# Two matrix layers that read their moving operand's 512 columns from two halves in turn

## The chip, the core and the metric

The kernel runs on one core of a Trainium2 chip. The engines named below are PE (TensorE: matmuls; its weight loads are listed apart as PEld), DVE (VectorE), ACT (ScalarE), POOL (GpSimd) and SP (SyncE, which issues the DMAs). The metric is the device time of one launch in microseconds, the median of several runs.

## What is computed

A linear recurrence over time (batch 4, 8 heads, 768 steps, 48 features per head) feeds a two-layer perceptron of 3072 tokens, 384 model features and 2048 hidden units:

```python
for t in range(S):
    cur = einsum('bhd,bhe->bhde', u * k[t], v[t])
    y[t] = einsum('bhd,bhde->bhe', r[t], state + cur)
    state = w * state + einsum('bhd,bhe->bhde', k[t], v[t])
x = y.transpose(0, 2, 1, 3).reshape(B * S, H * D)     # 3072 x 384
h = x @ w_in                                          # 3072 x 2048
g = 0.5 * h * (1 + erf(h / sqrt(2)))
out = g @ w_out                                       # 3072 x 384
```

## The kernel before

Time is cut into 6 chunks of 128 steps. A chunk has 4 x 128 = 512 tokens, and they are the 512 columns of every matmul of the perceptron, in the order batch, then time. The recurrence of a chunk is worked out in closed form for 4 pairs of heads ("groups", with the tiles `Tb`, `Nb`, `Am`, `Sa`, `Sb`, `cs` and the PSUM tiles `A` and `Y`). A group ends in `xx` (or `x3`), the perceptron's input of that chunk.

The hidden units are cut into 16 blocks of 128. One step m is one block of one chunk, 96 steps in all. Each factor is split into a high and a low part in the 4-byte type fp32r, and three products are added up: high x high, high x low, low x high. A step is therefore

- `product1`, 9 matmuls of 512 columns (3 products x 3 pieces of the 384 features) that add up in the PSUM tile `Hp`;
- on ACT, two passes of Gelu over `Hp`: `gh` (line 728, rounded to fp32r) and `gf` (line 729); on DVE `gl` = `gf` - `gh` (line 730);
- `product2`, 9 matmuls of 512 columns that read `gh` and `gl` and add up in the PSUM tiles `O0`, `O1`, `O2`. In the last chunk `O2`'s 512 columns are done as two matmuls of 256, the second half into `Y`.

On PE, `product2` of step m-1 stands behind `product1` of step m, so that Gelu is worked out under it. `Hp` is one tile: the next `product1` must wait until `gf` has read it. The weights (`wh`, `wl`) are loaded as 8-byte numbers and split once, in the 16 steps of the first chunk: on ACT lines 395, 398 and 404, on DVE lines 400 and 407. In that chunk DVE and ACT so do the weights' split beside Gelu and the next chunk's groups.

The order of all instructions is worked out before the launch by a planner (`Plan`). It holds a list of operations with an engine, an estimated duration, a due time and dependencies, and plays them through; what it starts first on an engine stands first in that engine's queue. `MM` is its duration of one matmul of 512 columns; it has no other use. The last line of `kernel` puts the output, written as chunk x feature x column, back in the order of tokens.

Of the kernel before, what the change touches and what calls it, by code (L numbers as in the profile page):

```python
# [21 lines left out]
B, H, S, D = 4, 8, 768, 48  # L22
DM, DF = 384, 2048
C = 128
NCH = S // C
# [14 lines left out]
FIRST, STEP, STEP_LAST = 27000, 8400, 3900  # L40
WEIGHT_AHEAD, GROUP_AHEAD, GROUP_DUE = 26000, 28000, 18000
LEFT = 6
HEATS, HEAT_NS, HEAT_ROOM, MM = 10, 300, 100, 233
WIDE = 96
POOL_DUE, POOL_CLASH = 8000, 550
LATER_BONUS = "d"
# [144 lines left out]
def rwkv_gelu_mlp(tc, rkT, rkv, wuT, uN, wmlp, r, k, vT, w, u, out):  # L191
    nc = tc.nc
    with ExitStack() as ctx:
# [61 lines left out]
        act = lambda n: 60 + n / 1.2  # L255
        pool = lambda n: 200 + n * 2.1

        flat2 = lambda x: x.rearrange("p a b c -> p (a b c)")
        slot = lambda gi: gi if gi < NP else NP + gi % 2

# [432 lines left out]
        def product1(x, j, n, ks=range(3), start=False, stop=False, dst=Hp):  # L693
            wt, a = ((wh, 0), (wl, 0), (wh, 1))[n]
            for k_ in ks:
                nc.tensor.matmul(dst, lhsT=wt[j][:, 0, k_ * 128:(k_ + 1) * 128], rhs=x[:, a, k_, :],  # L696
                                 start=start and k_ == ks[0], stop=stop and k_ == ks[-1])

        def hidden(m):
# [8 lines left out]
        def moe1(m, at):  # L708
            t, j = divmod(m, NJ)
            high, low, GH, GL = hidden(m)  # L710
            x, X = xx[t % 2], f"xx{t % 2}"

            xr = lambda a, ks=range(3): [f"{X}{k_}{a}" for k_ in ks]
            gaps = [f"{X}{k_}g{i}" for k_ in range(3) for i in range(2)]
            n1 = 2 * j
            dst, H_ = (O[2], "O2") if m == 1 else (Hp, "H")
            if m == 0:
                gaps0 = lambda k_: gaps[2 * k_:2 * k_ + 2]
                for k_ in range(3):
                    first = add("pe", 3 * MM, at + k_, lambda k_=k_: [  # L720
                        product1(x, j, n, (k_,), k_ == 0 and n == 0, k_ == 2 and n == 2) for n in range(3)],
                        r=["wh0", "wl0"] + xr("h", (k_,)) + xr("l", (k_,)) + gaps0(k_), w=["H"])
                    plan.heat_to = plan.heat_to or first
            else:
                for n in range(3):
                    add("pe", 3 * MM, at + n, lambda n=n: product1(x, j, n, start=n == 0, stop=n == 2, dst=dst),
                        r=[f"{('wh', 'wl', 'wh')[n]}{n1}"] + xr("hhl"[n]) + gaps, w=[H_])
            add("act", 480, LATER, lambda: nc.scalar.activation(out=high, in_=dst, func=AF.Gelu, scale=256.0), r=[H_], w=[GH])  # L728
            add("act", 480, LATER, lambda: nc.scalar.activation(out=gf, in_=dst, func=AF.Gelu, scale=256.0), r=[H_], w=["gf"])  # L729
            add("dve", dve(512), LATER, lambda: nc.vector.tensor_tensor(  # L730
                out=low, in0=gf, in1=high.bitcast(F32), op=ALU.subtract), r=["gf", GH], w=[GL], port=True)
# [5 lines left out]
        def product2(j, high, low, n, part):  # L737
            wt, gt = ((wh, high), (wl, high), (wh, low))[n]
            d, dst, a, b = part
            nc.tensor.matmul(dst[:, a:b], lhsT=wt[j][:, 1, d * 128:(d + 1) * 128], rhs=gt[:, a:b],  # L740
                             start=(j == 0 and n == 0), stop=(j == NJ - 1 and n == 2))

        def moe2(m, at, dest):
# [4 lines left out]
            def go(m, n, which, at):  # L748
                j = m % NJ
                high, low, GH, GL = hidden(m)  # L750
                add("pe", MM * sum(parts[i][3] - parts[i][2] for i in which) / TOK, at, lambda: [product2(j, high, low, n, parts[i]) for i in which],
                    r=[f"{('wh', 'wl', 'wh')[n]}{2 * j + 1}", (GH, GH, GL)[n]], w=[banks[i] for i in which])
# [164 lines left out]
        with tc.If(plain[0] < LP * NP):  # L917
            general = ctx.enter_context(ExitStack())
            xT = general.enter_context(tc.tile_pool(name="xT", bufs=1, space=bass.MemoryType.DRAM)).tile(
                [3, 128, NB, S], F32, name="xT")  # L920
            with ExitStack() as rec:
                recur(rec.enter_context(tc.tile_pool(name="rec", bufs=1)), xT)
            g = general.enter_context(tc.tile_pool(name="g", bufs=2))
            with tc.For_i(0, NCH, 1) as c:
                xf = g.tile([128, 3, NB, C], F32, name="xf")
                xhl = g.tile([128, 2, 3, TOK], F32R, name="xhl")
                for k_ in range(3):
                    nc.scalar.dma_start(xf[:, k_], xT[k_][:, :, ds(c * C, C)])
                xflat = xf.rearrange("p k b t -> p k (b t)")
                nc.scalar.copy(out=xhl[:, 0], in_=xflat)  # L930
                nc.vector.tensor_tensor(out=xhl[:, 1], in0=xflat, in1=xhl[:, 0].bitcast(F32), op=ALU.subtract)
                o = g.tile([128, 3, TOK], F32, name="og")
                for j in range(NJ):
                    for n in range(3):
                        product1(xhl, j, n, start=n == 0, stop=n == 2)
                    ghs, gfs, gls = (g.tile([128, TOK], dt, name=x) for x, dt in (("ghs", F32R), ("gfs", F32), ("gls", F32R)))
                    nc.scalar.activation(out=ghs, in_=Hp, func=AF.Gelu, scale=256.0)
                    nc.scalar.activation(out=gfs, in_=Hp, func=AF.Gelu, scale=256.0)
                    nc.vector.tensor_tensor(out=gls, in0=gfs, in1=ghs.bitcast(F32), op=ALU.subtract)
                    for n in range(3):  # L940
                        for part in PARTS:
                            product2(j, ghs, gls, n, part)
                for d in range(3):
                    nc.vector.tensor_scalar(out=o[:, d], in0=O[d], scalar1=256.0, scalar2=None, op0=ALU.mult)
                nc.scalar.dma_start(out[ds(c, 1)].rearrange("o d p n -> p (o d) n"), o)
            general.close()
# [61 lines left out]
```

## Time and profile before

| | |
|---|---|
| median of 3 runs | 478.93 us (478.82 to 479.67) |
| profiled execution, first to last instruction | 476.6 us |
| time outside the span, median less span | 2.3 us |
| PE busy | 469.2 us, 98% |
| DVE, ACT, POOL busy | 230.7, 181.8, 67.6 us |
| DMA | 46.6 MB, 98 GB/s in the mean |

The profile holds one execution; no device time of its own is given for it beside the span. A matmul's listed duration (393 to 398 ns for 512 columns) covers its whole way through the array and overlaps with the next one's. What a matmul costs in a stream is the distance from its start to the next one's start, which the timeline's start times give.

### The profile page before, as it was taken

The page shows a single profiled execution, that of the slowest core. Times are in us where ns is not written, and L with a number is a line of the kernel's source. Part 1 is how long each engine was busy: PE and PEld are TensorE (multiplying, and loading weights), DVE is VectorE, ACT ScalarE, POOL GpSimd, SP SyncE. Part 2 cuts the span into 40 slices and gives each one's busy share as a digit, 9 for nine tenths or more (in the row PEclk, how much of TensorE's full clock was granted, in tenths as well). Part 3 has the DMA queues.
Part 4 walks back from the last instruction along what each step waited for, and adds up shares of the span by engine and source line. Part 5 has one row for each costly group of instructions (what it writes and reads, how often), then busy time and mean ns, then how long its engine had stood idle before and what let it go on. Part 6 is the DMA issues. An engine that isn't in the chain of part 4 may idle for free.

```text
span 476.6 us, 10284 instructions
## 1 busy us (share of the span) xinstructions
PE 469.2 (98%) x4525; PEld 378.3 (79%) x4525; DVE 230.7 (48%) x345; ACT 181.8 (38%) x333; POOL 67.6 (14%) x91
## 2 busy tenths in 40 slices
PE   8999999999999999999999999999999999999996
PEld 6767788888888787888888888888888887888875
DVE  7989989754354266153543543544435311211111
ACT  9998897233222223222223222223322222322221
POOL 1331021221020222010202202202112000000000
PEclk9999999999999999999999999999999999999999
DMA  8978682414023034031231330321402000100002
GB/s 306 362 296 312 231 265 91 122 48 155 25 83 106 2 114 153 1 106 39 69 106 67 96 99 9 106 54 52 162 15 91 14 0 12 66 1 1 1 0 72
DMA packets 15426, 46.60 MB, mean 98 GB/s; under 512 B 3664, under 2 KB 4048, under 8 KB 15376
## 3 DMA queue, kind: packets, MB, share of 16 engines
q1 hardware_dynamic: 15376, 45.88, 28.8%
q8 instruction: 37, 0.61, 0.5%
q14 instruction: 13, 0.11, 0.1%
HBM read 38.73 MB, written 4.72 MB: 91 GB/s over the span
## 4 chain that ended last, share of the span: by engine, by line
PE 92%; DMA 4%; ACT 3%; issue 0%; DVE 0%; ACTq 0%
PE Hp L696 42%; PE O L740 41%; PE Y L606 2%; DMA E<-W 2%; PE A L614 2%; PE Y L634 2%; PE A L623 1%; DMA raw<-in_wmlp_dram 1%; PE Y L740 1%; ACT W L344 0%; ACT Sa L530 0%; ACT wa L312 0%; ACT L291 0%; ACT wa L395 0%; ACT gh L728 0%; ACT gf L729 0%
## 5 line engine op out<-in xcount | busy, mean ns | idle before, releaser
L696 PE MATMUL Hp<-xx,wh 128*128 128x512 f32 x570 | 167.2, 401 | 0.0
L730 DVE TENSOR_TENSOR gl<-gf,gh 128x512 fp32r<-128x512 f32 x92 | 66.9, 727 | 166.4 <-ACT gf L729 166.1
L728 ACT ACTIVATE gh<-Hp 128x512 fp32r<-128x512 f32 x91 | 54.4, 598 | 213.9 <-PE Hp L696 213.8
L696 PEld LDWEIGHTS Hp<-xx,wh 128*128 128x128 f32 x570 | 104.4, 188 | 25.8 <-ACT gf L729 1.5
L696 PE MATMUL Hp<-xx,wl 128*128 128x512 f32 x285 | 82.1, 395 | 0.0
L740 PE MATMUL O<-gh,wh 128*128 128x512 f32 (+1 forms) x276 | 78.6, 391 | 0.5 <-ACT gf L729 0.5
L740 PE MATMUL O<-gh,wl 128*128 128x512 f32 (+1 forms) x276 | 78.6, 391 | 0.0
L740 PE MATMUL O<-gl,wh 128*128 128x512 f32 (+1 forms) x276 | 78.3, 390 | 0.0
L696 PEld LDWEIGHTS Hp<-xx,wl 128*128 128x128 f32 x285 | 53.6, 188 | 12.7
L740 PEld LDWEIGHTS O<-gh,wh 128*128 128x128 f32 x276 | 51.7, 188 | 13.5 <-ACT gf L729 0.9
L740 PEld LDWEIGHTS O<-gh,wl 128*128 128x128 f32 x276 | 51.2, 188 | 11.6
L740 PEld LDWEIGHTS O<-gl,wh 128*128 128x128 f32 x276 | 51.0, 188 | 11.4 <-issue 0.2
L729 ACT ACTIVATE gf<-Hp 128x512 f32<-128x512 f32 x95 | 56.3, 593 | 0.0
L561 POOL TENSOR_TENSOR Nb<-Nb 128x384 f32<-128x384 f32 x20 | 20.4, 1018 | 124.7 <-DMA Nb<-in_rkv_dram 75.4
L558 DVE TENSOR_TENSOR Tb<-Tb,E 112x1024 f32<-112x1024 f32 x20 | 25.4, 1268 | 2.3 <-DMA Tb<-in_rkT_dram 2.3
L663 DVE SCALAR_TENSOR_TENSOR Sb<-Sa,E,A 48x192 f32<-48x192 f32 x40 | 16.5, 413 | 18.1 <-PE A L623 17.5
L433 ACT CAST xx<-Y 112x512 fp32r<-112x512 f32 x15 | 8.8, 587 | 38.8 <-PE Y L634 38.7
L564 POOL TENSOR_TENSOR Nb<-Nb,WN 128x384 f32<-128x384 f32 x20 | 20.3, 1016 | 21.2 <-DVE wl L407 7.8
L567 POOL TENSOR_TENSOR Nb<-Nb,u_sb 128x384 f32<-128x384 f32 x20 | 20.3, 1013 | 17.8 <-DVE gl L730 12.5
L570 DVE TENSOR_REDUCE cs<-Nb 128x8 f32<-128x384 f32 x20 | 11.1, 553 | 18.1 <-POOL Nb L567 15.8
L644 POOL MEMSET done<- 1x1 f32 x19 | 1.7, 89 | 124.6 <-PE Y L606 124.6
L670 DVE COPY_PREDICATED Am<-past,A 128x512 f32<-128x512 uint32 x20 | 14.9, 747 | 7.0 <-PE A L623 6.8
(124 smaller groups left out, 388.9 us busy)
## 6 DMA issues: line engine op xcount, KB each, us to landing
raw<-in_wmlp_dram SPq DMA_DIRECT2D x16, 767.8 KB, 6.6
Nb<-in_rkv_dram SPq DMA_DIRECT2D x20, 576.0 KB, 5.6
Tb<-in_rkT_dram SPq DMA_DIRECT2D x20, 512.0 KB, 4.1
out_dram<-raw SPq DMA_DIRECT2D x5, 768.0 KB, 3.6
T<-in_rkT_dram SPq DMA_DIRECT2D x4, 512.0 KB, 5.0
xx<-x SPq DMA_DIRECT2D x30, 64.0 KB, 4.2
N<-in_rkv_dram SPq DMA_DIRECT2D x4, 384.0 KB, 7.0
out_dram<-raw SPq DMA_DIRECT2D x2, 256.0 KB, 2.1
```

What stands on the lines that cost most here:

```text
L558: add("dve", 1140, LATER, lambda: nc.vector.tensor_tensor(out=flat, in0=flat, in1=E[:, p, 0].rearrange("l h i -> l (h i)").unsqueeze(1).to ...
L561: add("pool", pool(DM), LATER, lambda: nc.gpsimd.tensor_tensor(out=n[:, 0], in0=n[:, 0], in1=n[:, 1], op=ALU.mult), r=[NK], w=[NR])
L564: add("pool", pool(DM), LATER, lambda: nc.gpsimd.tensor_tensor(out=kn, in0=kn, in1=WN2[:, p].rearrange("s j d -> s (j d)").unsqueeze(1).to ...
L567: add("pool", pool(DM), LATER, lambda: nc.gpsimd.tensor_tensor(out=n[:, 0], in0=n[:, 0], in1=u_sb[:, p, :].unsqueeze(1).to_broadcast([C, N ...
L570: add("dve", 465, LATER, lambda: nc.vector.tensor_reduce(out=sums, in_=n[:, 0].rearrange("s b (j d) -> s (b j) d", d=D), axis=AX.X, op=ALU ...
L663: add("dve", 430, at, lambda l=l, x=x: nc.vector.scalar_tensor_tensor(out=out[quarter(1 - x)], in0=src[l], scalar=E[l, p, 1, h, 32:33], in ...
L670: add("dve", 625, LATER, lambda: nc.vector.copy_predicated(out=am, mask=past2.bitcast(U32).unsqueeze(1).unsqueeze(1).to_broadcast([C, 2, N ...
L696: nc.tensor.matmul(dst, lhsT=wt[j][:, 0, k_ * 128:(k_ + 1) * 128], rhs=x[:, a, k_, :], start=start and k_ == ks[0], stop=stop and k_ == ks ...
L728: add("act", 480, LATER, lambda: nc.scalar.activation(out=high, in_=dst, func=AF.Gelu, scale=256.0), r=[H_], w=[GH])
L729: add("act", 480, LATER, lambda: nc.scalar.activation(out=gf, in_=dst, func=AF.Gelu, scale=256.0), r=[H_], w=["gf"])
L730: add("dve", dve(512), LATER, lambda: nc.vector.tensor_tensor(out=low, in0=gf, in1=high.bitcast(F32), op=ALU.subtract), r=["gf", GH], w=[G ...
L740: nc.tensor.matmul(dst[:, a:b], lhsT=wt[j][:, 1, d * 128:(d + 1) * 128], rhs=gt[:, a:b], start=(j == 0 and n == 0), stop=(j == NJ - 1 and ...
```

## The change

The moving operand of every matmul of both layers is read through a view in which column 2n is column n of the tile and column 2n + 1 is column 256 + n: two 4-byte numbers 1 KiB apart, then the next two. The weights' reads and the PSUM writes keep their form. `product1` so writes `Hp` with its tokens shuffled once, Gelu keeps that order, and `product2` shuffles them again. Two such shuffles of 512 = 4 x 128 columns turn the order batch, time into time, batch, and the last line of `kernel` reads the output in that order. The halves of `O2` in the last chunk take 128 pairs each. The number of matmuls, weight loads, DMAs and bytes, and every instruction of ACT, DVE and POOL, stays the same. `MM` goes from 233 to 216, and with it the order that the planner finds.

```diff
-HEATS, HEAT_NS, HEAT_ROOM, MM = 10, 300, 100, 233
+HEATS, HEAT_NS, HEAT_ROOM, MM = 10, 300, 100, 216
...
+        pairs = lambda x: x.rearrange("p (a n) -> p n a", a=2)
...
-                nc.tensor.matmul(dst, lhsT=wt[j][:, 0, k_ * 128:(k_ + 1) * 128], rhs=x[:, a, k_, :],
+                nc.tensor.matmul(dst, lhsT=wt[j][:, 0, k_ * 128:(k_ + 1) * 128], rhs=pairs(x[:, a, k_, :]),
...
-            nc.tensor.matmul(dst[:, a:b], lhsT=wt[j][:, 1, d * 128:(d + 1) * 128], rhs=gt[:, a:b],
+            nc.tensor.matmul(dst[:, a:b], lhsT=wt[j][:, 1, d * 128:(d + 1) * 128], rhs=pairs(gt)[:, a // 2:b // 2],
...
-    got = res.results[0]["out_0_dram"].reshape(NCH, DM, B, C)
-    return np.ascontiguousarray(got.transpose(2, 0, 3, 1).reshape(B * S, DM))
+    got = res.results[0]["out_0_dram"].reshape(NCH, DM, C, B)
+    return np.ascontiguousarray(got.transpose(3, 0, 2, 1).reshape(B * S, DM))
```

With the new `MM` the planner moves instructions in the first chunk and at the start of the second and third; behind that the engines' orders are the same. Line numbers of the changed kernel are higher by one from line 258 on. On PE the first place is step 1 of the first chunk, whose `product1` goes to `O2` (`O_72` below; `O_70` and `O_71` are `O0` and `O1`; `wh_74` and `wl_78` are block 0's weights, `wh_75` and `wl_79` block 1's). Before:

```order
L696 MATMUL O_72<-xx_121,wh_75 128x512 x3
L696 MATMUL O_72<-xx_121,wl_79 128x512 x3
L696 MATMUL O_72<-xx_121,wh_75 128x512 x3
L740 MATMUL O_70<-gh_124,wh_74 128x512
L740 MATMUL O_71<-gh_124,wh_74 128x512
L740 MATMUL O_70<-gh_124,wl_78 128x512
```

And of the change:

```order
L697 MATMUL O_72<-xx_121,wh_75 128x512 x3
L741 MATMUL O_70<-gh_124,wh_74 128x512
L741 MATMUL O_71<-gh_124,wh_74 128x512
L697 MATMUL O_72<-xx_121,wl_79 128x512 x3
L697 MATMUL O_72<-xx_121,wh_75 128x512 x3
L741 MATMUL O_70<-gh_124,wl_78 128x512
```

Two matmuls of `product2` have moved ahead of the six of `product1` that need `wl_79` and the low part of `xx`.

On DVE the second place is where the first later group (`Nb_111`, `cs_117`) meets the splits of the weights (`wb`, `wl`). Before:

```order
L407 TENSOR_TENSOR wl_80<-wb_136,wh_76 128x768
L663 SCALAR_TENSOR_TENSOR Sb<-Sa,E,A 48x192 x2
L663 SCALAR_TENSOR_TENSOR Sa<-Sb,E,A 48x192
L570 TENSOR_REDUCE cs_117<-Nb_111 128x8
L663 SCALAR_TENSOR_TENSOR Sa<-Sb,E,A 48x192
L577 TENSOR_TENSOR Am_113<-diag_85,cs_117 128x512
L400 ISA wb_134<-wb_134,wa_133 128x1536
L670 COPY_PREDICATED Am_113<-past_86,A 128x512
L730 TENSOR_TENSOR gl_126<-gf,gh_124 128x512
L407 TENSOR_TENSOR wl_81<-wb_134,wh_77 128x768
```

And of the change:

```order
L408 TENSOR_TENSOR wl_80<-wb_136,wh_76 128x768
L571 TENSOR_REDUCE cs_117<-Nb_111 128x8
L664 SCALAR_TENSOR_TENSOR Sb<-Sa,E,A 48x192
L578 TENSOR_TENSOR Am_113<-diag_85,cs_117 128x512
L664 SCALAR_TENSOR_TENSOR Sb<-Sa,E,A 48x192
L671 COPY_PREDICATED Am_113<-past_86,A 128x512
L664 SCALAR_TENSOR_TENSOR Sa<-Sb,E,A 48x192 x2
L401 ISA wb_134<-wb_134,wa_133 128x1536
L731 TENSOR_TENSOR gl_126<-gf,gh_124 128x512
L401 ISA wb_135<-wb_135,wa_132 128x1536
```

The group's `Am` is finished before two of the state updates, and `wl_81` has moved behind one more `wb`; the same instructions stand there in another order.

## Rows read from the trace of the kernel before

**Rows 1.** The page: span, and busy time of each engine.
```profile
span 476.6 us, 10284 instructions
PE 469.2 (98%) x4525; PEld 378.3 (79%) x4525; DVE 230.7 (48%) x345; ACT 181.8 (38%) x333; POOL 67.6 (14%) x91
```

**Rows 2.** The page: shares of the chain that ended last, by engine and line.
```profile
PE 92%; DMA 4%; ACT 3%; issue 0%; DVE 0%; ACTq 0%
...
PE Hp L696 42%; PE O L740 41%; PE Y L606 2%; DMA E<-W 2%; PE A L614 2%; PE Y L634 2%; PE A L623 1%; DMA raw<-in_wmlp_dram 1%; PE Y L740 1%; ACT W L344 0%; ACT Sa L530 0%; ACT wa L312 0%; ACT L291 0%; ACT wa L395 0%; ACT gh L728 0%; ACT gf L729 0%
```

**Rows 3.** The waits of PE: us in total, times, longest us.
```profile
PE A L305 <- DVE W L321: 1.6, 1, 1.6
PE O L740 <- ACT gf L729: 0.5, 1, 0.5
```

**Rows 4.** Timeline of PE in the fourth chunk: start us, us, engine, line, operation.
```profile
301.16 0.86 PE L696 MATMUL Hp<-xx,wl 128*128 128x512 f32 x3
...
304.65 0.86 PE L696 MATMUL Hp<-xx,wh 128*128 128x512 f32 x3
...
308.16 0.86 PE L740 MATMUL O<-gl,wh 128*128 128x512 f32 x3
```

**Rows 5.** Timeline of PE in the last chunk, one product2 with matmuls of 256 columns.
```profile
429.91 0.75 PE L740 MATMUL O<-gh,wh 128*128 128x512 f32 x3
430.49 0.28 PE L740 MATMUL Y<-gh,wh 128*128 128x256 f32 x1
430.61 0.75 PE L740 MATMUL O<-gh,wl 128*128 128x512 f32 x3
...
432.01 0.85 PE L696 MATMUL Hp<-xx,wh 128*128 128x512 f32 x3
```

**Rows 6.** Timeline of PE in the first 7 us.
```profile
2.58 1.05 PE L305 MATMUL Y<-zeros 128*128 128x512 f32 x2
...
4.71 1.05 PE L305 MATMUL A<-zeros 128*128 128x512 f32 x2
...
6.80 0.55 PE L354 MATMUL O<-ident,W 112*128 112x112 f32 x4
```

**Rows 7.** Windows: PE, PEld, DVE, ACT, POOL busy us, granted clock, DMA share, GB/s.
```profile
440.00:450.00 10.00, 10.00 (x52) 8.40 (x51) 1.69 (x3) 2.18 (x4) 0.00 (x0) 1.00 0.01 2
...
45.00:60.00 15.00, 15.00 (x64) 11.69 (x64) 14.28 (x18) 13.36 (x20) 1.47 (x2) 1.00 0.71 252
...
23.00:100.00 77.00, 76.39 (x897) 60.30 (x894) 68.60 (x92) 57.20 (x85) 18.05 (x22) 1.00 0.62 214
100.00:450.00 350.00, 349.89 (x3314) 283.56 (x3313) 137.78 (x214) 96.55 (x177) 45.36 (x59) 1.00 0.20 62
```

**Rows 8.** Groups of PE's instructions by line and form: count, busy us, mean ns.
```profile
L696 PE MATMUL Hp<-xx,wh 128*128 128x512 f32 x570 | 167.2, 401 | 0.0
L696 PE MATMUL Hp<-xx,wl 128*128 128x512 f32 x285 | 82.1, 395 | 0.0
...
L354 PE MATMUL O<-ident,W 112*128 112x112 f32 x4 | 0.5, 259 | 0.0
```

**Rows 9.** Groups of ACT's instructions by line and form.
```profile
L398 ACT ACTIVATE wb<-raw 128x768 int32<-128x768 uint32 x16 | 14.6, 910 | 3.5 <-DMA raw<-in_wmlp_dram 2.1 <-DVE wl L407 1.4
L404 ACT CAST wh<-wb 128x768 fp32r<-128x768 f32 x16 | 13.1, 834 | 1.6 <-DVE wb L400 1.6
```

**Rows 10.** Timeline of ACT, the second Gelu pass of two steps.
```profile
303.25 0.59 ACT L729 ACTIVATE gf<-Hp 128x512 f32<-128x512 f32 x1
...
455.10 0.59 ACT L729 ACTIVATE gf<-Hp 128x512 f32<-128x512 f32 x1
```

**Rows 11.** Timeline of PE near the end, where products are held back.
```profile
454.41 0.63 PE L740 MATMUL O<-gh,wh 128*128 128x512 f32 x2
...
455.81 0.91 PE L696 MATMUL Hp<-xx,wh 128*128 128x512 f32 x3
```

## The prediction

> **What bounds the kernel now.** I read four views in turn. The page's busy times come first: PE is busy for 469.2 of 476.6 us, and DVE, the next engine, for 48% [rows 1]. A busy PE need not be a bound one, so the chain of waits comes second. It runs through PE for 92% of the span, and through the two lines of the perceptron, `product1` (L696) and `product2` (L740), for 42% and 41% [rows 2]. Third, PE's own waits: the largest is 1.6 us at the start, and behind the first steps there is none [rows 3]. So PE is fed without gaps, and what a matmul costs in the stream decides the time.
>
> That cost is read from the start times in the timeline. From 301.16 to 308.16 us PE starts ten triples of matmuls, alternately of both layers, which is 30 matmuls in 7.00 us or 233.3 ns each [rows 4]. The granted clock there is 1.00, the level of 2.4 GHz [rows 7]. A column per clock would make 512 columns 213.3 ns, so 20.0 ns or 9.4% are lost on each matmul. What are they? Three readings narrow it down.
>
> - They go with the columns, not with the instructions. In the last chunk a `product2` of twelve matmuls with 4608 columns runs from 429.91 to 432.01 us; nine matmuls of 512 columns take 9 x 233.3 = 2100 ns, the same [rows 5]. A cost per matmul or per weight load would have shown as a longer time there.
> - The neighbours don't make them. From 100 to 450 us, where rows 4 stand, DVE is busy for 39% of the time and DMA for 20%; from 440 to 450 us, like rows 5 in the last chunk, it is 17% and 1%, and a column costs the same [rows 4, 5, 7].
> - They are not there at half the pace. The five warm-up matmuls from 2.58 to 4.71 us, also 512 contiguous columns of a 4-byte type, take 426 ns each: a column per 0.83 ns, 1.2 columns per ns [rows 6]. The four fp32 transposes of 112 columns take 0.55 us together and the last of them 0.259, which leaves 97 ns between starts: two clocks of 2.4 GHz a column make 93.3 [rows 6, 8].
>
> So the loss appears where one row of memory is walked through at 2.4 columns a ns, and is absent where it is walked through at 1.2.
>
> **The change, part by part.** The view of two halves makes each half be walked through at 1.2 columns a ns, while together they give 2.4. If the loss belongs to the walk through neighbouring addresses, it goes. Then a matmul costs between 213.3 ns (the warm-up matmuls show nothing beside their columns) and 217 ns (the transposes show 3.7 ns beside theirs). I take 215.5, the middle, a gain of 17.8 ns.
>
> How many matmuls are these? `product1` has 570 + 285 = 855 into `Hp` [rows 8], 95 steps x 9, and step 1's nine into `O2`, 864 in all; `product2` has the columns of another 864. The gain is 1728 x 17.8 = 30.8 us.
>
> What of it reaches the end? Everything on PE that gets shorter must not run into what it waits for.
>
> - Chunks 2 to 5: the next `product1` waits for `gf`. It ends at 303.25 + 0.59 = 303.84 and PE comes at 304.65, so 0.81 us are to spare [rows 4, 10]. `product2` between them shrinks by 9 x 17.8 = 160 ns, and 0.65 us stay. DVE and ACT are busy for 39% and 28% from 100 to 450 us [rows 7]. Nothing is lost.
> - First chunk: 16 steps save 16 x 18 x 17.8 = 5.1 us, and the stretch from 23 to 100 us would shrink from 77 to 71.9. DVE has 68.60 us of work in it, 95.4% of the shorter stretch, and the densest piece seen, 45 to 60 us, has 14.28 of 15, or 95.2% [rows 7]. The weights' splits can't be put off, since each step needs its block. So the gain just fits, at the edge. What is lost lies between nothing and the whole 5.1. I take 1.3, a quarter, since the stretch as a whole fits to within 0.2 us, while ACT is dense in the same piece too (13.36 of 15). The moved instructions (two matmuls ahead of six on PE, another order of splits and group work on DVE) add no work and are counted in this term.
> - End: in four of the last steps `product2` has only six matmuls, and `gf` ends at 455.10 + 0.59 = 455.69, 0.12 us before PE comes at 455.81 [rows 10, 11]. Six matmuls shrink by 107 ns, so 0.01 is left. Whether PE can follow so closely is not shown; the cost is between 0 and 4 x 0.107 = 0.43 us, and I take 0.2.
> - Gelu, `gl` and the copies out read and write contiguous rows as before, whatever tokens stand in them; the output is one DMA of the same size. The new order costs nothing on the chip.
>
> Sum: -30.8 + 1.3 + 0.2 = -29.3 us. The profiled span becomes 447.3 us. The profile's span is 2.3 us below the median of the runs, and what lies outside it doesn't change: 478.9 - 29.3 = **449.6 us**. With all bounds on one side it is 478.9 - 1728 x 20.0 / 1000 = 444.3, on the other 478.9 - 30.8 + 5.1 + 0.4 = 453.6, with a matmul at 215.5.
>
> **The rivals.**
>
> *Each hop costs (slower).* Every column now comes from another place than the one before, 1 KiB away. No row shows PE reading so. The nearest row is ACT's: line 398 reads every second 4-byte word, 768 of them, in 910 ns, and line 404 reads 768 contiguous ones in 834 [rows 9], which is 0.10 ns a word. Added to each column, 512 x 0.10 = 51 ns make a matmul 284 ns and the kernel 478.9 + 1728 x 0.051 = 567 us. The far end is PE's half pace of rows 6: 426 ns a matmul, +333 us, 812 us. It decides from a hop of 0.04 ns a column, since the loss that can be won is 20.0 / 512. For it: ACT's rows. Against it: ACT's row strides within one walk and converts a type besides, and it has no two halves of which one can rest while the other is read.
>
> The Trainium skill speaks for this rival: "SBUF — State Buffer", section "Door 1: The DMA port swizzle", says that consecutive accesses to the same 16-byte line go at full bandwidth and that each access which crosses to a new line pays. Contiguous 4-byte columns cross at every fourth column, the changed ones at every column, so by that rule the loss would grow, to the 567 us or beyond. This trace agrees with it only in that the loss goes with the columns; it does not show that the crossing itself is what costs, and the matmuls at half pace cross as often per column and lose nothing.
>
> *A part of the loss goes.* If half of it stays, the gain is 15.4 us and the time 463.5; an early stage that loses its whole 5.1 us beside it makes this 468.
>
> *Nothing moves (no change).* The 233.3 ns could be the rate at which PE's read path or its PSUM write gives 4-byte columns, 2.19 a ns, from wherever they come. Rows 5 and 6 fit that as well. Then only the planner's new order is left, which adds no instruction; PE stays fed as in rows 3, and the time is 478.9.
>
> **How the numbers follow.** The whole loss goes: 0.70. A part of it: 0.14. No change: 0.05. Slower: 0.11. I give the first most weight, because a loss that is the same whatever runs beside it and vanishes at half pace looks like one place asked again too soon, and alternating asks each place half as often. The likeliest case gives 449.6, with its own range from 444.3 to 453.6. To hold 8 in 10 the range must take in most of the partial case, so it goes from 445 to 470. A measurement here tells 0.2%, about 1 us, from no change. Faster has 0.84, the first two cases; within 0.2% 0.05; slower 0.11.
>
> **What would show it.** Right: starts of triples 0.645 to 0.651 us apart in place of 0.700, the same for both layers and all chunks, the 256-column matmuls shorter in proportion; no wait of PE on ACT or DVE of more than 1 to 2 us in all from 23 to 100 us; DVE at 93% or more there; waits of PE for `gf` near the end of a tenth of a us each. Wrong: triples at 0.700 (no change), at 0.67 (a part), or above 0.75 (hops cost); or triples at 0.65 with PE waiting for several us in the first chunk, which would mean that the early stage is bound by DVE and ACT and the saving there was not to be had.

## The result and the profile after

The changed kernel takes 454.35 us in the median (453.82 to 454.99, 4 runs) beside 479.3 us for the kernel before (478.82 to 479.85, 4 runs): 0.948 times as long [0.9465, 0.9494]. It is faster by 25 us; the forecast was 29.3.

The page of the changed kernel gives its span and busy times, and the chain that ended last by engine and line:

```profile
span 452.1 us, 10289 instructions
...
PE 440.6 (97%) x4525; PEld 379.4 (84%) x4525; DVE 229.4 (51%) x345; ACT 186.7 (41%) x333; POOL 68.5 (15%) x91
...
PE 78%; ACT 8%; DVE 6%; DMA 5%; issue 2%; POOL 1%; SPq 0%; ACTq 0%; POOLq 0%
PE Hp L697 36%; PE O L741 34%; DMA E<-W 2%; PE Y L607 2%; ACT wh L405 2%; ACT wa L396 2%; PE Y L635 2%; PE A L615 2%; ACT wb L399 1%; DVE wb L401 1%; DMA raw<-in_wmlp_dram 1%; PE Y L741 1%; PE A L624 1%; DMA T<-in_rkT_dram 1%; ACT gh L729 1%
```

PE is 28.6 us shorter than in [rows 1], and its share of the chain is no longer 92% as in [rows 2]. ACT and DVE have come in with the weights' split (`wa`, `wb`, `wh`). ACT itself is busy for 4.9 us more than in [rows 1], with the same 333 instructions.

The timeline of PE in the fourth chunk, beside [rows 4]:

```profile
316.07 0.81 PE L697 MATMUL Hp<-xx,wh 128*128 128x512 f32 x3
316.72 0.81 PE L697 MATMUL Hp<-xx,wl 128*128 128x512 f32 x3
...
319.31 0.81 PE L741 MATMUL O<-gl,wh 128*128 128x512 f32 x3
```

Five triples lie between the first and the last start: 3.24 us, or 216 ns a matmul, where [rows 4] gave 233.3. Over the whole trace the start times give 215.9, and 233.25 before. For 1728 matmuls that makes 30.0 us. How much of it has arrived is seen from the start of every sixteenth step and of the last matmul, read from both timelines:

| start of | before, us | after, us | saved | possible |
|---|---|---|---|---|
| step 0 | 23.6 | 23.7 | -0.1 | 0 |
| step 16 | 101.0 | 102.1 | -1.1 | 5.0 |
| step 32 | 178.4 | 170.9 | 7.5 | 10.0 |
| step 48 | 252.3 | 241.8 | 10.5 | 15.0 |
| step 64 | 327.7 | 312.2 | 15.5 | 20.0 |
| step 80 | 402.65 | 382.12 | 20.5 | 25.0 |
| last matmul | 471.8 | 446.8 | 25.0 | 30.0 |

By step 48, 4.5 us are gone; from there to step 80 every chunk saves its full 5.0; the last one loses 0.5. The rows of steps 16 and 32 can't be taken as they stand: ahead of step 16 the new order has one `product2` more (nine matmuls, 1.9 us), ahead of step 32 it has 128 of the groups' short matmuls fewer (1.9 us); at step 48 both orders are level. So I also added up, from all of PE's start times, what each interval is longer than the steady one. In the first chunk this excess is 2.9 us before and 6.6 after, so 3.7 of the loss were made there. The rest is 0.3 from step 16 to step 80, 0.7 from there to the last matmul, and 0.3 in the groups' own matmuls.

The waits of PE (us in total, times, longest):

```profile
PE O L741 <- ACT gh L729: 2.5, 4, 1.0
PE A L306 <- DVE W L322: 1.6, 1, 1.6
PE O L741 <- ACT gf L730: 0.8, 1, 0.8
...
PE Hp L697 <- ACT gf L730: 0.4, 1, 0.4
```

[Rows 3] had no wait for `gh`. The timeline of PE shows three of the new waits:

```profile
26.78 0.81 PE L697 MATMUL O<-xx,wh 128*128 128x512 f32 x3
27.95 0.70 PE L741 MATMUL O<-gh,wh 128*128 128x512 f32 x2 [0.36 <-ACT gh L729]
...
31.60 0.48 PE L741 MATMUL O<-gh,wh 128*128 128x512 f32 x1 [0.80 <-ACT gf L730]
...
36.77 0.81 PE L697 MATMUL Hp<-xx,wh 128*128 128x512 f32 x3
38.27 0.92 PE L741 MATMUL O<-gh,wh 128*128 128x512 f32 x3 [0.69 <-ACT gh L729]
```

The first is at the two matmuls that the new order moved ahead. At 38.27 `product2` stands directly behind `product1` of its own step, so that PE stands still while Gelu runs. What takes ACT longer than before is seen in its groups from 23 to 102 us, beside [rows 9]:

```profile
L396 ACT ACTIVATE wa<-raw 128x768 f16<-128x768 bf16 x14 | 16.7, 1195 | 0.2 <-DMA raw<-in_wmlp_dram 0.2
L399 ACT ACTIVATE wb<-raw 128x768 int32<-128x768 uint32 x14 | 16.7, 1223 | 0.2 <-DVE wl L408 0.2
L405 ACT CAST wh<-wb 128x768 fp32r<-128x768 f32 x15 | 12.4, 834 | 3.6 <-DVE wb L401 3.6
```

Line 399, which was line 398, took 910 ns before and takes 1223 now. Line 396 took 1094 ns (as line 395, with the old reading in the new order) and takes 1195. Both read every second 4-byte word, or one 2-byte number in 8 bytes. Line 405 reads neighbouring words and stays at 834. Before the perceptron starts, the same line 399 still takes 0.93 and 0.94 us (at 16.71 and 21.94 us), so it is slow only beside the new matmuls.

The windows (columns as in [rows 7]) show which engine is dense now:

```profile
23.00:45.00 22.00, 19.65 (x301) 15.36 (x297) 18.77 (x26) 19.65 (x28) 7.76 (x8) 1.00 0.79 278
45.00:60.00 15.00, 14.09 (x64) 11.82 (x65) 14.46 (x20) 14.61 (x20) 1.01 (x1) 1.00 0.73 252
60.00:80.00 20.00, 19.58 (x231) 16.51 (x233) 16.66 (x24) 18.80 (x24) 4.13 (x5) 1.00 0.56 202
80.00:97.00 17.00, 16.89 (x307) 14.73 (x298) 13.28 (x21) 8.26 (x14) 4.51 (x6) 1.00 0.36 106
97.00:430.00 333.00, 332.89 (x3341) 289.76 (x3340) 142.67 (x221) 98.38 (x180) 46.93 (x60) 1.00 0.22 67
```

From 45 to 60 us ACT is busy for 14.61 of 15, where it had 13.36, and PE for 14.09 in place of 15.00. From 97 to 430 us PE lacks nothing. The granted clock is 1.00 in all five, the level of 2.4 GHz, as in [rows 7].

One thing in front of the prediction has to be put right: on PE the order changed in the last steps too. Between the last five `product1`s stood six matmuls of `product2` each time; now 8, 8, 8 and 7 stand there, counted in 512 columns.

### The profile page after: what moved, and what is told of

The parts are those of the page before. It is cut to its first block, busy times and chain, and to the rows that moved or that the text cites. A ratio compares the mean times of both kernels' runs of the same rounds, so it can differ in the third digit from the quotient of the medians.

```text
span 452.1 us, 10289 instructions
## 1 busy us (share of the span) xinstructions
PE 440.6 (97%) x4525; PEld 379.4 (84%) x4525; DVE 229.4 (51%) x345; ACT 186.7 (41%) x333; POOL 68.5 (15%) x91
## 4 chain that ended last, share of the span: by engine, by line
PE 78%; ACT 8%; DVE 6%; DMA 5%; issue 2%; POOL 1%; SPq 0%; ACTq 0%; POOLq 0%
PE Hp L697 36%; PE O L741 34%; DMA E<-W 2%; PE Y L607 2%; ACT wh L405 2%; ACT wa L396 2%; PE Y L635 2%; PE A L615 2%; ACT wb L399 1%; DVE wb L401 1%; DMA raw<-in_wmlp_dram 1%; PE Y L741 1%; PE A L624 1%; DMA T<-in_rkT_dram 1%; ACT gh L729 1%
## 5 line engine op out<-in xcount | busy, mean ns | idle before, releaser
L697 PE MATMUL Hp<-xx,wh 128*128 128x512 f32 x570 | 157.0, 383 | 0.4 <-ACT gf L730 0.4
L741 PE MATMUL O<-gh,wh 128*128 128x512 f32 (+1 forms) x276 | 74.5, 377 | 3.3 <-ACT gh L729 2.5
L697 PE MATMUL Hp<-xx,wl 128*128 128x512 f32 x285 | 77.4, 379 | 0.0
L741 PE MATMUL O<-gl,wh 128*128 128x512 f32 (+1 forms) x276 | 74.1, 376 | 0.0
L741 PE MATMUL O<-gh,wl 128*128 128x512 f32 (+1 forms) x276 | 73.9, 375 | 0.0
L568 POOL TENSOR_TENSOR Nb<-Nb,u_sb 128x384 f32<-128x384 f32 x20 | 21.3, 1064 | 6.7 <-DVE gl L731 6.7
L571 DVE TENSOR_REDUCE cs<-Nb 128x8 f32<-128x384 f32 x20 | 11.0, 552 | 21.4 <-POOL Nb L568 20.5
L396 ACT ACTIVATE wa<-raw 128x768 f16<-128x768 bf16 x16 | 18.9, 1182 | 0.2 <-DMA raw<-in_wmlp_dram 0.2
L399 ACT ACTIVATE wb<-raw 128x768 int32<-128x768 uint32 x16 | 18.6, 1187 | 0.2 <-DVE wl L408 0.2
```

The source lines that it names most:

```text
L396: add("act", 930, LATER, lambda: nc.scalar.activation(out=a.bitcast(F16).rearrange("p (n t) -> p n t", t=2)[:, :, 1], in_=top.bitcast(BF16 ...
L399: add("act", 815, LATER, lambda: nc.scalar.activation(out=b, in_=rest.bitcast(U32), func=AF.Copy, scale=2.0 ** -13), r=[R_], w=[B_])
L568: add("pool", pool(DM), LATER, lambda: nc.gpsimd.tensor_tensor(out=n[:, 0], in0=n[:, 0], in1=u_sb[:, p, :].unsqueeze(1).to_broadcast([C, N ...
```

## The experiments

Two theories stand for the lost 5 us. **A**: ACT's strided reads get slower while PE reads two distant places in turn, and the first chunk is too dense to take it. **B**: the planner's new order is at fault. Two more stand for what the reading itself does. **P**: what counts is that neighbouring columns come from different lines of 16 bytes. **Q**: the two places must lie in different large banks. E and D follow further down.

**order_only**: the old reading in the new order.

```diff
-HEATS, HEAT_NS, HEAT_ROOM, MM = 10, 300, 100, 233
+HEATS, HEAT_NS, HEAT_ROOM, MM = 10, 300, 100, 216
```

> The planner's new order alone, with the moving columns read in a row as before. Theory A (the two-halves reading by PE slows ACT's strided reads of the weights, lines 395 and 398, and this costs the first chunk its gain): the time stays at that of before within 1.5 us, line 398 stays at 0.90 to 0.93 us and line 395 at 1.09. Theory B (the new order of the first chunk costs the gain, by about 5 us): 484 us, with step 16 starting near 106 us instead of 101.

Measured: 480.77 us beside 478.69, 1.004 times [1.0024, 1.0056], so 2.1 us more. PE's waits:

```profile
PE O L740 <- ACT gh L728: 1.9, 3, 0.7
```

The new order alone makes PE wait for Gelu, with matmuls as long as before and with line 398 at its old 902 ns. That is more than A alone allows and less than B foretold. Step 16 starts at 105.8 us, as B said, but 1.0 us of that is there at step 0 already, and 2.1 are the `product2` that the new order has ahead of it.

**halves_old_order**: the new reading in the order of before.

```diff
-HEATS, HEAT_NS, HEAT_ROOM, MM = 10, 300, 100, 216
+HEATS, HEAT_NS, HEAT_ROOM, MM = 10, 300, 100, 233
```

> The two-halves reading with the planner's order of before. Theory A: the strided reads are slow again, 1.15 to 1.25 us at line 399 and 1.15 to 1.2 at line 396, step 16 starts at 101 to 103 us, and the time is 453 to 456. Theory B: step 16 starts near 97 us and the time is about 449.5.

Measured: 455.53 beside 478.69, 0.952 times [0.950, 0.954]. Lines 399 and 396 are slow here too (1167 and 1197 ns from 23 to 102 us), so this hangs on the reading and not on the order; step 16 starts at 101.3 us, and both numbers are A's. PE waits 1.7 and 1.1 us for `gf` and 0.9 for `gh`. The old order loses 1.2 us more than the new one once the matmuls are short.

**first_contig**: the first chunk reads contiguously and is planned with 233 ns a matmul, the others read from two halves (the general view that later kernels share is shown here).

```diff
-        pairs = lambda x: x.rearrange("p (a n) -> p n a", a=2)
+        def pairs(x, t, a=0, b=TOK):
+            mode = MODES[t]
...
+            return x.rearrange("p (h a n) -> p h n a", a=2, n=mode)[:, a // (2 * mode):b // (2 * mode)]
```

> The first chunk reads its columns in a row at 233 ns a matmul (and is planned so), the five others read two halves. Theory A: the strided ACT reads are back at 0.91 and 1.09 us, step 16 starts at about 101 us as before, and the time is some 1 us below the change, 453.3. If the strided reads stay at 1.2 us with PE reading in a row, theory A falls.

Measured: 454.87, 0.950 times [0.948, 0.952]. ACT's groups from 23 to 102 us:

```profile
L408 ACT ACTIVATE wa<-raw 128x768 f16<-128x768 bf16 x14 | 15.1, 1091 | 1.1 <-DMA raw<-in_wmlp_dram 1.1
L411 ACT ACTIVATE wb<-raw 128x768 int32<-128x768 uint32 x15 | 13.6, 907 | 2.6 <-DVE wl L420 2.6
```

ACT's durations came back, as A said. The time missed its number by 1.6 us: the slower matmuls of this chunk cost what ACT gave back.

**row_words_halves**: line 399 reads 768 words in a row instead of every second one, and so leaves out the weights' low bits.

```diff
-            rest = flat2(raw[j % 3]).rearrange("p (n t) -> p n t", t=2)[:, :, 0]
+            rest = flat2(raw[j % 3])[:, 0:2 * DM]
```

> The change, with one ACT read of the weights (line 399) taking 768 words that lie in a row instead of every second one; the weights' low bits are wrong by this. Theory A: line 399 falls to 0.83 to 0.92 us while line 396, still strided, stays at 1.19; ACT's work in the first chunk falls by about 4.5 us, step 16 starts at 98 to 100 us and the time is 450 to 452. Theory B: line 399 is shorter too or not, but step 16 and the time stay within 1 us of the change.

Measured: 453.04, 0.948 times [0.944, 0.953]. ACT's groups from 23 to 102 us:

```profile
L396 ACT ACTIVATE wa<-raw 128x768 f16<-128x768 bf16 x14 | 16.8, 1200 | 0.5 <-DMA raw<-in_wmlp_dram 0.4
L399 ACT ACTIVATE wb<-raw 128x768 int32<-128x768 uint32 x15 | 12.7, 866 | 0.3 <-DVE wl L408 0.3
```

The line that reads in a row is quick beside the same matmuls, the other one is not: the stride of ACT's own read is needed for the slowdown. In time this is 1.3 us by the medians, less than A expected and within the interval of the change.

**row_words_before**: the same edit in the kernel before.

> The kernel before with line 398 reading 768 words in a row (the weights' low bits are wrong by this). Theory A: line 398 goes from 0.91 to 0.83 to 0.86 us, a small step, since no two-halves reading slows it, and the time stays within 1.5 us of before; PE has no waits to win back there.

Measured in one run: 479.28 beside 479.76, with line 398 at 846 ns. Beside contiguous matmuls there is little to win from it.

**distances** and **hops**: the two places lie another distance apart in each chunk, and from the second chunk on one more ACT operation a step reads a spare tile, in four forms by turns.

```diff
+MODES = (256, 128, 64, 32, 16, 8)
```
```diff
+MODES = (256, "s2", 4, "q4", 2, 0)
...
+            if mode == "s2":
+                return x.rearrange("p (n a) -> p a n", a=2)
+            if mode == "q4":
+                return x.rearrange("p (a n) -> p n a", a=4)
```

`s2` reads all even columns and then all odd ones; `q4` takes the four quarters in turn; 0 is contiguous.

> The two places that are read in turn lie 256 columns apart in the first chunk and then, chunk by chunk, 128, 64, 32, 16 and 8 columns (blocks of twice that width). From the second chunk on each step has one more ACT read of a spare tile after Gelu: in turn every second 4-byte word, words in a row, every fourth 2-byte word, every fourth 4-byte word. Theory P (one place of memory asked again too soon, each place walked at half the pace): 216 ns a matmul at every distance that leaves the place, so at least at 128 and 64 columns, and 233 from some shorter distance on. Theory Q (the two halves must lie in different large banks): 216 at 256 alone, or down to one distance, 233 or more below. On ACT, theory A expects the strided reads at 1.2 us wherever the matmul is at 216 ns, and 0.83 to 0.91 for words in a row.

> By chunk: 256 columns apart; all even columns and then all odd ones; places 4 columns apart; four quarters in turn; places 2 columns apart; columns in a row. The same extra ACT reads. Theory P: four quarters 216 ns; 2 apart 233, since both columns are mostly in the same place; even-then-odd is a walk through one place and stays at 233 or gets worse, as it covers the memory twice as fast. If each hop cost something by itself, even-then-odd and four quarters would be slower than 216 by the same amount. Theory A expects the strided ACT reads at 0.91 us in the last chunk, where PE reads in a row, and at 1.2 in the chunk of the quarters.

Measured in one run each: 454.08 beside 479.76, and 551.77. PE's timeline of hops, in the order even-then-odd, 4 apart, quarters, 2 apart:

```profile
161.96 1.54 PE L709 MATMUL Hp<-xx,wl 128*128 128x512 f32 x3
163.32 1.54 PE L709 MATMUL Hp<-xx,wh 128*128 128x512 f32 x3
...
260.17 0.81 PE L753 MATMUL O<-gh,wh 128*128 128x512 f32 x3
260.82 0.81 PE L753 MATMUL O<-gh,wl 128*128 128x512 f32 x3
...
351.07 1.02 PE L709 MATMUL Hp<-xx,wl 128*128 128x512 f32 x3
351.92 1.02 PE L709 MATMUL Hp<-xx,wh 128*128 128x512 f32 x3
...
430.62 0.86 PE L709 MATMUL Hp<-xx,wl 128*128 128x512 f32 x3
431.32 0.86 PE L709 MATMUL Hp<-xx,wh 128*128 128x512 f32 x3
```

A third of the distance between two starts is the matmul's cost: 453, 217, 283 and 233 ns. Over all matmuls of a pattern:

| columns are read | ns a matmul |
|---|---|
| contiguously | 233 |
| from two places 256, 128, 64, 32, 16, 8 or 4 columns apart | 216 |
| from two places 2 columns apart | 233 |
| from the four quarters in turn | 283 |
| all even, then all odd | 453 |

Q falls: 4 columns, which are 16 bytes, do as well as 256. P has its border in the right place and allowed for a loss in even-then-odd, but it gave the quarters 216 ns too; in that form it falls. What fits all five rows is that it matters how many lines of 16 bytes are read in turn, and how many columns each of them gives. The mechanism isn't shown.

The same runs tell when ACT suffers. ACT's groups of distances while PE's places are 64 columns apart (175 to 241 us), then 32 columns (247 to 312 us); line 907 reads every second word, 909 words in a row, 911 one 2-byte number in 8 bytes, 913 every fourth word:

```profile
L911 ACT ACTIVATE wa<-raw 128x768 f16<-128x768 bf16 x4 | 5.0, 1246 | 0.0
L907 ACT ACTIVATE wb<-raw 128x768 int32<-128x768 uint32 x4 | 4.9, 1216 | 0.4 <-DVE Sa L676 0.4
L913 ACT ACTIVATE wb<-raw 128x384 int32<-128x384 uint32 x3 | 3.6, 1214 | 0.0
L909 ACT ACTIVATE wb<-raw 128x768 int32<-128x768 uint32 x4 | 3.4, 846 | 0.0
...
L911 ACT ACTIVATE wa<-raw 128x768 f16<-128x768 bf16 x4 | 4.3, 1087 | 0.0
L909 ACT ACTIVATE wb<-raw 128x768 int32<-128x768 uint32 x4 | 3.4, 846 | 0.0
L907 ACT ACTIVATE wb<-raw 128x768 int32<-128x768 uint32 x3 | 2.8, 933 | 0.0
L913 ACT ACTIVATE wb<-raw 128x384 int32<-128x384 uint32 x3 | 2.8, 927 | 0.0
```

At 64 columns (and at 128: 1146, 1233, 1214 ns) the three strided reads are slow; at 32 and at all shorter distances, quarters and contiguous reading they take 904 to 933 ns (907, 913) and 1082 to 1094 (911). Line 909 takes 845 to 852 everywhere. So PE can have its 216 ns without ACT's loss. A had expected slow reads wherever a matmul takes 216 ns, and beside the quarters; in that form it falls.

**near16** and **near4**: 16 and 4 columns apart in all chunks, in the order of the change.

```diff
+MODES = (16, 16, 16, 16, 16, 16)
```

> The change with its two places 16 columns apart in place of 256, in all chunks; the order of all instructions is that of the change. Theory A2 (the slowed strided ACT reads are what delays Gelu in the first chunk): a matmul takes 216 ns, line 395's and 398's reads are back at 0.91 and 1.09 us, ACT has some 6 us less to do in the first chunk, PE's waits for Gelu there fall from about 4.7 us to 1 to 2, and the time is 450 to 451.5. Theory C (the first chunk is bound by DVE and ACT together, or by the order, whatever the strided reads take): the reads are short again but PE waits for 3.5 us or more and the time is 453 to 454.5.

> The same with places 4 columns, 16 bytes, apart. Both theories: the same time as at 16 columns within 1 us, a matmul at 216 ns.

Measured: near16 452.14 beside 479.07, 0.944 times [0.9427, 0.9453], and near4 452.71, 0.946 [0.944, 0.948]. The interval of near16 doesn't touch that of the change: it beats both kernels. ACT's groups from 23 to 102 us in near16:

```profile
L408 ACT ACTIVATE wa<-raw 128x768 f16<-128x768 bf16 x14 | 15.2, 1084 | 0.5 <-DMA raw<-in_wmlp_dram 0.5
L411 ACT ACTIVATE wb<-raw 128x768 int32<-128x768 uint32 x15 | 13.5, 918 | 0.5 <-DVE wl L420 0.5
```

And PE's waits there:

```profile
PE O L753 <- ACT gh L741: 2.1, 4, 0.7
...
PE O L753 <- ACT gf L742: 0.5, 1, 0.5
```

ACT's strided reads are back at their old time, and A's part of the loss is measured: 2.2 us by the medians. The time lies between what A2 (450 to 451.5) and C (453 to 454.5) had named. By the traces the excess of the first chunk falls from 6.6 to 5.3, 1.3 us. But before had 2.9, and PE's waits for `gh` remain.

**near16_old_order**: near16 with `MM` at 233.

> Places 16 columns apart with the planner's order of before; the fourth corner beside the change (new order, 256 apart), the old order at 256 and the new order at 16. If the order and the slowed ACT reads cost independently, it is some 2 us below the old order at 256 columns apart, about 453.5. If the new order were what makes PE wait for Gelu in the first chunk, it would reach 449 to 450.

Measured: 455.42, 0.950 times [0.947, 0.954]; PE waits 2.2 us for `gf` and 0.6 for `gh`. With short matmuls the new order is better by 3.3 us at 16 columns and by 1.2 at 256 (455.53 to 454.35): beside the old order B falls, though the new one has its own waits.

What are the remaining waits? **E**: they come with the order, where `product2` stands right behind its own step's `product1`, so that Gelu's latency lies bare. **D**: DVE has too much work in this stretch and comes late. Too much work for ACT is tried first.

**no_gf_first**: the change, with the second Gelu pass cut to 8 columns in the first chunk, which leaves out `gl` there.

```diff
+            nc_ = TOK if t else 8
-            add("act", 480, LATER, lambda: nc.scalar.activation(out=gf, in_=dst, func=AF.Gelu, scale=256.0), r=[H_], w=["gf"])
+            add("act", 480, LATER, lambda: nc.scalar.activation(out=gf[:, 0:nc_], in_=dst[:, 0:nc_], func=AF.Gelu, scale=256.0), r=[H_], w=["gf"])
+            g2 = gf if t else high.bitcast(F32)
```

> The change (256 columns apart), with the second Gelu pass of the first chunk cut from 512 columns to 8 and its result not used, so that the low part of the hidden layer is zero there; the order stays. ACT has about 6 us less to do, and the strided reads stay slow. Theory A2: relief of ACT is what counts, wherever it comes from, and the time is 450 to 451.5. Theory C in the form that DVE binds: 453.5 to 454.5, with DVE over 95% from 24 to 80 us.

Measured: 452.43, 0.946 times [0.943, 0.948]. ACT's groups from 23 to 102 us:

```profile
L399 ACT ACTIVATE wb<-raw 128x768 int32<-128x768 uint32 x15 | 17.5, 1195 | 0.6 <-DVE wl L408 0.6
...
L731 ACT ACTIVATE gf<-Hp 128x8 f32<-128x8 f32 x15 | 2.8, 190 | 0.0
```

PE's waits:

```profile
PE O L743 <- ACT gh L729: 2.6, 4, 1.1
```

ACT has 15 x (593 - 190) ns = 6 us less to do, its strided reads are as slow as in the change, and the time is that of near16. So giving ACT room wins about the 2 us that giving its reads their old pace wins, though the interval overlaps that of the change too, and 6 us of room win no more than that. DVE is busy for 49.02 of 56 us from 24 to 80, 88%, so it is not at the 95% that C wanted. The waits for `gh` are as long as in the change.

**near16_less_dve**: near16, with DVE's scaling of `Tb` cut to an eighth in the first groups; the rest of `Tb` is left unscaled.

```diff
+            nr = 1 if gi < 10 else 2 * NB
-                out=flat, in0=flat, in1=E[:, p, 0].rearrange("l h i -> l (h i)").unsqueeze(1).to_broadcast(
-                    [LP, 2 * NB, C]), op=ALU.mult), r=EVERY, w=[TR], port=True)
+                out=flat[:, 0:nr], in0=flat[:, 0:nr], in1=E[:, p, 0].rearrange("l h i -> l (h i)").unsqueeze(1).to_broadcast(
+                    [LP, nr, C]), op=ALU.mult), r=EVERY, w=[TR], port=True)
```

> Places 16 columns apart, order of the change, with DVE's scaling of the rows of the groups that stand in the first chunk cut from 1024 columns to 128 (the rest stays unscaled), some 6 us less DVE work there. Theory D (with the ACT reads short again, DVE's work binds the first chunk): PE's waits fall by 2 us or more and the time is 449.5 to 450.5. Theory E (the order itself makes PE follow Gelu too closely, four times): the waits of PE for Gelu stay at about 2.6 us and the time stays within 1 us of the same kernel with the whole DVE work, 452.1.

Measured: 452.42, 0.943 times [0.940, 0.946]. The window from 24 to 60 us in near16 (columns as in [rows 7]):

```profile
24.00:60.00 36.00, 33.37 (x358) 26.90 (x354) 32.00 (x44) 31.47 (x46) 7.72 (x8) 1.00 0.77 275
```

The same window of this kernel:

```profile
24.00:60.00 36.00, 33.52 (x360) 27.02 (x355) 29.50 (x44) 31.51 (x46) 7.73 (x8) 1.00 0.76 274
```

Its waits of PE:

```profile
PE O L754 <- ACT gh L742: 2.0, 3, 0.7
...
PE O L754 <- ACT gf L743: 0.5, 1, 0.5
```

DVE has 2.5 us less to do and nothing moves. D falls here, and more room for ACT didn't help these waits in no_gf_first; E is left. One of the waits shows it, in the timeline of near16:

```profile
38.16 0.60 ACT L741 ACTIVATE gh<-Hp 128x512 fp32r<-128x512 f32 x1 [1.07 <-PE Hp L709]
...
38.81 0.92 PE L753 MATMUL O<-gh,wh 128*128 128x512 f32 x3 [0.69 <-ACT gh L741]
```

ACT has been idle for 1.07 us, and PE waits for the 0.60 us of `gh` alone. This wait is 0.69 us in the change, order_only, near4, no_gf_first and near16_less_dve too, whatever ACT and DVE have to do beside it; before, halves_old_order and near16_old_order don't have it. Whether an order that keeps another step's matmuls between the two layers would win these 2 us was not tried.

A run's time also holds what comes before step 0, which starts at 23.6 to 24.8 us in these traces, and behind the last matmul's start, 4.6 to 6.0 us. Between the two starts the traces, one of each kernel, give:

| kernel | us from step 0 to the last matmul |
|---|---|
| before | 448.2 |
| order_only | 449.9 |
| the change | 423.1 |
| halves_old_order | 424.7 |
| near16 | 421.2 |
| near16_old_order | 423.6 |
| row_words_halves | 421.5 |
| no_gf_first | 421.5 |

The old pace of the strided reads so wins 1.9 us, and row_words_halves has 1.6 of them, clearer than in the medians. The new order costs 1.7 us with the old reading and wins 1.6 and 2.4 with the new one.

## Why the prediction was right, and where it was short

- **What bounds it.** PE's stream did, and its intervals set the time: right. The loss that goes with the columns went with the reading: 233.25 to 215.9 ns. I had taken 215.5, and 17.8 ns in place of 17.35, 0.8 us too much over 1728 matmuls.
- **Why it is 216 ns.** I gave the whole loss most weight because it looked "like one place asked again too soon, and alternating asks each place half as often". Four quarters ask each place a quarter as often and take 283 ns, so this reason doesn't hold as I gave it. The number was right; why two places are quicker stays open, and so far it was luck.
- **Chunks 2 to 5.** "Nothing is lost": right from step 48 to step 80, with 5.0 of 5.0 us in both chunks; from step 16 to step 48 PE's intervals lose 0.3.
- **First chunk.** This is the mis-sized term: 1.3 us taken, 3.7 measured there (4.5 by step 48), near its upper bound of 5.1. Two things were wrong in its working. That every instruction of ACT stays the same holds for their number, not for their length: by the traces 1.3 of the 3.7 us went to the strided reads, which near16 wins back (1.9 with what follows behind the chunk). And that the moved instructions "add no work and are counted in this term" passed over that they uncover Gelu's latency: order_only shows 1.7 us from it, and near16 still has 2.4 us more excess than before. The price was also worked out from DVE, with ACT as a mere addition. DVE was to be at 93% or more from 23 to 100 us; the windows from 23 to 97 us give it 63.17 of 74 us, 85%. ACT was the denser one from 45 to 80 us: 14.61 of 15 and 18.80 of 20 us, DVE 14.46 and 16.66. One sign of being wrong came in part: triples at 0.65 us with PE waiting for 3.7 us in the first chunk (2.5, 0.8 and 0.4), where 1 to 2 were allowed.
- **End.** 0.2 us taken, 0.7 measured on PE. The matmuls of 256 columns go from 116.3 to 110.3 ns and not in proportion to 107.6, which is 0.3 us. Four intervals of 294 to 306 ns stand in the last steps where 216 would, and before there were four of 275 to 282 where 233 would; that is 0.1 us more, and the rest is spread in small pieces. The path that I had priced, `product1` waiting for `gf` behind six matmuls, doesn't occur: the new order has 7 or 8 there, and PE has no wait for `gf` behind the first chunk. Another 0.5 us came behind PE, where I had set nothing: from the last matmul's start to the end it is 5.29 us in place of 4.75. The first three output DMAs take SP's queue 2.69 us to issue (444.96 to 447.65) in place of 2.19, and the last one follows at 447.76, 0.95 us behind that start in place of 0.80. The other 0.4 isn't explained; near16, whose order is the same, takes 4.81. The span shrank by 24.5 us while the last matmul starts 25.0 earlier.
- **The sum.** -30.0 + 3.7 + 0.3 + 0.7 + 0.3 + 0.5 = -24.5, the span's difference, beside the forecast of -29.3. The measured 454.35 us lies in the range from 445 to 470, but 0.75 us beyond 453.6, the likeliest case with all bounds on one side. The first chunk stayed within its bound; what carried the time over it are the smaller gain, the terms that I had at nothing (0.3 from step 16 to 80, 0.3 in the groups, 0.5 behind PE), the end, and a kernel before of 479.3 us in place of 478.9.
- **The rival "each hop costs".** Not for this change: 216 ns, although every column comes from another place. Other patterns do cost more than reading in a row: 283 ns from four quarters and 453 for even-then-odd. The Trainium skill's rule of "SBUF — State Buffer", section "Door 1: The DMA port swizzle", that each crossing to a new line of 16 bytes pays, agrees with these two in that they lose, and not with the change, which crosses at every column and gains. Nor do the sizes follow it: the quarters cross at every column and lose 50 ns, even-then-odd crosses at every second and loses 220.
- **"Nothing moves"** falls with 216 ns: the 233.3 ns were not the rate of the read path or of the PSUM write wherever the columns come from.

## What to carry to other kernels

An fp32r matmul whose columns cost more than a clock each in the stream can be worth reading from two places in turn; take them near each other (16 columns here), and look at what strided readers on other engines take beside it. When a bound engine gets faster, the stage that was already dense gives nothing for free: count there who is late next, on each engine, with durations taken beside the new work. And a planner's new duration is a change of its own, to be run alone.

## What the runs showed of the hardware

- fp32r matmuls over 512 contiguous columns start 233 ns apart at a granted clock of 1.00; read in turn from two places 4 to 256 columns apart 216 ns, from four quarters 283, all even columns and then all odd ones 453.
- ACT's strided SBUF reads take 1146 to 1246 ns in place of 904 to 1094 while PE alternates between two places 64 columns (256 bytes) or more apart, and no longer than usual at 32 columns (128 bytes) or less, or beside four quarters in turn; reads of neighbouring words stay at 834 to 866. "SBUF — State Buffer" of the Trainium skill, section "Who interferes with whom", says that only the port pair shared by DVE and GpSimd causes contention. These traces show another slowdown, of ACT's reads beside PE's; what the two share isn't shown.
